# Moving the waits for a q tile's six loads from the first max matmuls to the o products ahead of them

## The chip, the cores and the metric

The kernel runs on one core of one Trainium2 chip. The metric is the device time of one execution in microseconds (us); lower is better. The time before is a median over three runs. One further execution was taken with the hardware profiler, and all durations below are read from its trace.

Five engines work in parallel, each with its own in-order stream of instructions: PE (matmuls, with its weight loads shown as a row of their own, PEld), DVE (vector), ACT (activations), POOL and SP, which here only issues DMAs. They are held together by semaphores. An instruction of PE can carry one semaphore to wait for. Where it depends on more, the build puts one or two instructions ahead of it in PE's stream that do nothing but wait; the trace shows them as EVENT_SEMAPHORE in the row PEldq.

## The reference, cut to what matters

The output mixes two branches of the same input x (1 x 2048 x 640) by a gate g = sigmoid(x . gate_w):

```
def _A_ref(x, wq, wk, wv, wo):            # 32 heads of 20, one k and one v for all heads
    ...
    scores = jnp.einsum("bhqd,bkd->bhqk", q, k) * (Dh ** -0.5)
    p = _softmax(scores, axis=-1)
    o = jnp.einsum("bhqk,bkd->bhqd", p, v)
    return (...o...) @ wo
def _B_ref(x, w1, b1, w2, b2):            # an MLP across the tokens
    h = _layernorm(x, axis=-1)
    u = _gelu(jnp.einsum("bsd,sf->bdf", h, w1) + b1)
    y = jnp.einsum("bdf,fs->bds", u, w2) + b2
    ...
return g * a + (1 - g) * b
```

Branch A is the larger part of the work: for every query and head a row of 2048 scores, its maximum, its exponentials and the product of these with v.

## The kernel before, in words

**Tiles.** A q tile holds 512 queries of four heads; there are NU = 32 of them. It is a pair of rows of blocks in SBUF: partitions 0 to 59 for two of the heads and 64 to 123 for the other two (three copies of 20 rows each, high, low and high part of q). `load_q(n)` fills it by six DMAs, which `part` issues on SP's queue (line 148), three for each half of the partitions. Each tile is used twice. First come its *max tiles* (`ms_next`, line 506): 64 matmuls of 128 queries by 512 keys, 32 with each half of the partitions, whose row maxima DVE takes (line 514). Later come its *score tiles* (`qk`, line 688), 128 keys by 512 queries, whose exponentials ACT writes to SBUF (line 700). Between the two the maxima go through DRAM and into two spare rows of the tile. So a tile's loads and the first max matmul of each half are tied by three DMA semaphores.

**Stretches and bursts.** The program is built in `n_st` stretches. A stretch j takes 8 score tiles, some 8 or 9 max tiles and a share of other work (the MLP's matmuls, lines 1008 and 836, later the product with wo, line 961), and places these on two lanes, the upper and the lower 64 rows of the array, whose matmuls run side by side. The order comes from `arrange`, `layout` and the cost model in `issue`; it is fixed when the program is built. After each stretch but the first, `burst` multiplies the exponentials of the two units of the previous stretch with v: eight matmuls at line 721 (`pv_mm`), which use all 128 rows and four column tiles of 32. They accumulate in one bank that ACT then copies out. PE alternates stretch, burst, stretch, burst.

**Waits.** `touch` (line 464) records by hand which instruction wrote or read a PSUM bank or a region of exponentials, and adds only the waits that follow from that. The waits for q tiles aren't in it; the framework adds them to the first instruction that reads the loaded rows.

**How many max tiles a stretch gets.** `wants[j]` plus what the last stretch left over; the two halves share them so that they keep in step (lines 1228 to 1235). `given[b]` counts the max tiles handed out for each half, so `given[b] // 32` is the q tile that half b is at.

In this text, the k-th burst is counted from 0, and the stretch after it has the same number.

Of the kernel before, what the change touches and what calls it, by code (L numbers as in the profile page):

```python
# [19 lines left out]
S, D, H, DH, F = 2048, 640, 32, 20, 1728  # L20
# [19 lines left out]
def mix_kernel(ctx: ExitStack, tc: tile.TileContext, A_x, A_wq, A_wk, A_wv, A_wo,  # L40
               B_x, B_w1, B_b1, B_w2, B_b2, gate_w, out):
    nc = tc.nc
    x = A_x[0]
    y_out = out[0]

    def f32(ap):
        return ap.bitcast(F32)
# [84 lines left out]
    def load_q(n):  # L132
        if n in FIFTH[:2]:
            t = w1b[3].rearrange("p r c f -> p r (c f)")
        elif n == 29:
            t = pools["q5"] = pools["last"].tile([P, 2, NB], F32R, name="q5")
        elif n in FIFTH or n in (6, 11, 16, 21, 26, 31):
            t, at = (slot[1], 2 * DC * D + 2 * D) if n in FIFTH else (slot[0], 2 * FC * HD2)
            t = t[:, at:at + 2 * NB].rearrange("p (r q) -> p r q", r=2)
        else:  # L140
            t = qp.tile([P, 2, NB], F32R, name="q")
        qb, g = divmod(n, NQ)
        cols = slice(qb * NB, (qb + 1) * NB)

        def part(b, j, src):
            o = 64 * b + DH * j
            rows = q_scr[src, g * 4 * DH:(g + 1) * 4 * DH, cols]
            nc.sync.dma_start(out=f32(t[o:o + DH]), in_=rows.rearrange("(a b d) q -> b d a q", a=2, b=2)[b])

        parts = [lambda b=b, j=j, src=src: part(b, j, src) for b in range(2) for j, src in enumerate((0, 1, 0))]  # L150
        if one_by_one[0]:
            q_parts_due.extend(parts)
        else:
            for f in parts:
                f()
        return t

    qtiles = {}
    one_by_one, q_parts_due = [False], []

    def new_q(n):
# [11 lines left out]
    with tc.tile_pool(name="pa", bufs=1) as pa, \  # L173
# [22 lines left out]
        for c in range(DC):  # L196
            nc.sync.dma_start(out=xin[0][:, :, c * P:(c + 1) * P],
                              in_=x[:NB, c * P:(c + 1) * P].rearrange("(t p) d -> p t d", p=P))
# [6 lines left out]
        for c in range(DC):  # L205
# [5 lines left out]
                          in_=B_b1[:(FC - 1) * P].rearrange("(c p) -> c p", p=P))  # L211
# [93 lines left out]
        def q_parts(m, ts):  # L305
            cols = slice(m * P, (m + 1) * P)
            return [[(wq_hi[:, c, cols], ts[c][0]) for c in range(DC)],
                    [(wq_hi[:, c, cols], ts[c][1]) for c in range(DC)],
                    [(wq_lo[:, c, cols], ts[c][0]) for c in (0, 3, 1, 4, 2)]]
# [88 lines left out]
        for sb in range(NQB):  # L398
# [11 lines left out]
            for m in range(DC):  # L410
# [3 lines left out]
                p = q_parts(m, ts)  # L414
# [46 lines left out]
    turns, xs, pre = [0], [], []  # L461
    writer, readers, engines = {}, {}, set()

    def touch(ins, reads=(), writes=()):
        need = []
        for r in reads:
            need.append(writer[r])
            readers.setdefault(r, []).append(ins)
        for w in writes:
            need += readers.pop(w, [])  # L470
            writer[w] = ins
        for n in {n.ins.name: n for n in need}.values():
            tc.add_manual_dep(ins.ins, n.ins.name, SYNC, reason="a bank or a p region used again")
        me = str(ins.ins.engine)
        engines.add(me)
        for e in engines - {me}:
            tc.declare_no_dep(ins.ins, group=e, keep=[n.ins for n in need], reason="other banks and p regions")
        tc.add_to_no_dep_group(me, ins.ins)

    def bank(i):  # L480
        return span(i, 1) if i < 7 else xs[2]
# [7 lines left out]
    given = [0, 0]  # L489
    issued = [0, 0]  # L490

    def ms_next(b):
        k = given[b]
        if k >= 32 * NU or k // 32 not in qtiles:
            return None
        given[b] += 1
        n, r = divmod(k, 32)
        (kq, pr), qt = divmod(r // 4, 2), r % 4

        def step(i=None):  # L500
            if n not in mtiles:
                mtiles[n] = mpool.tile([P, 16, 4], F32, name="mp")
            if i is None:
                turns[0] += 1
            ms = pre[turns[0] % 4].tile([P, NB], F32, name="x" if turns[0] % 4 else "g") if i is None else bank(i)
            mm = nc.tensor.matmul(ms, qtiles[n][64 * b:64 * b + 60, pr, qt * P:(qt + 1) * P],  # L506
                                  kst[64 * b:64 * b + 60, kq * NB:(kq + 1) * NB], start=True, stop=True)
            region = [("x", i)] if i is not None else []
            if region:
                touch(mm, writes=region)  # L510
            out = mtiles[n][:, (2 * b + pr) * 4 + qt, kq:kq + 1]

            def reduce():
                red = nc.vector.tensor_reduce(out, ms, axis=AX.X, op=ALU.max)  # L514
                if region:
                    touch(red, reads=region)
                issued[b] += 1

            return reduce

        return step
# [85 lines left out]
    with tc.tile_pool(name="psb", bufs=2, space=PSUM, side="right") as psb, \  # L607
# [13 lines left out]
        for fc in range(PRO):  # L621
            pu = [psb.tile([P, NB], F32, name=f"pu{r}") for r in range(2)]
            for hf in range(4):
# [4 lines left out]
                for c in range(HS):  # L628
                    st = hf * HS + c
                    for k, (w, h) in enumerate(((wh, h_hi[0]), (wh, h_lo[0]), (wl, h_hi[0]))):  # L630
                        for r in range(2):
                            rows = slice(64 * r, 64 * r + 64)
# [82 lines left out]
    osum = {}  # L715
    later = []

    def pv_mm(u, o, first, last, i):
        for hh in range(4):
            j = ptiles.pop((u, hh))  # L720
            mm = nc.tensor.matmul(o[32 * hh:32 * hh + 32, :], v_sb[:, units[u][1], :], p_all[:, j * NB:(j + 1) * NB],  # L721
                                  start=first, stop=last, skip_group_check=True)
            touch(mm, [("p", j)], [("x", i)])
            p_left[j // 4] -= 1
            if not p_left[j // 4]:
                p_free.append(j // 4)
# [316 lines left out]
    ph = [(rows[1 - b], rest if b else [], done if b else []) for rows, rest, done in seq for b in range(2)]  # L1043
    assert len(ph) == n_st
    first_use, last_use = {}, {}
    for i, (fs, _, _) in enumerate(ph):
        for f in fs:
            c = getattr(f, "chunk", None)
# [6 lines left out]
    for c in range(4 * PRO + 4, len(chunks)):  # L1055
        b = min((b for b in range(4) if b < 3 or last_use[c] < begin or over[3] >= ending - 1), key=lambda b: over[b])
# [10 lines left out]
    X_US, F_US, O_US = 0.2345, 0.1468, 0.869  # L1067
# [12 lines left out]
    def next_free():  # L1080
        return min(range(len(free)), key=lambda i: free[i])
# [102 lines left out]
    def burst(us):  # L1184
        i = next_free()
        t = max(max(lane) + FIRST_US, state["last"] + LAST_US, free[i]) + len(us) * O_US
        o = bank(i)
        for u in us:
            pv_mm(u, o, u == us[0], u == us[-1], i)
            fetch_at(u)  # L1190
        collect(us[-1], o, i)
        each, hold = EACH["act"]
        free[i] = spend("act", each, t + 0.25) - each + hold
        lane[:] = [t + NEXT_US] * 2
        fresh[:] = [True, True]
# [15 lines left out]
    wants = [8 + (len(fs) > 22) for fs, _, _ in ph]  # L1211
# [5 lines left out]
    left, n = 64 * NU - 16 - sum(given) - sum(wants[:at]), n_st - at  # L1217
    wants[at:] = sorted(left * (i + 1) // n - left * i // n for i in range(n))
    assert sum(given) + sum(wants[:n_st - 8]) >= 64 * (NU - 1)
    owed = 0  # L1220
    for j in range(n_st):
        h, i = j % 2, j // 2
        due, stores[:] = stores[:], []
        blocks = [], []
        ss = [lambda at, u=u, pr=pr: qk(u, pr, h, at, blocks[u % 4 // 2], pairs.get(2 * (u % 4) + pr, 1))
              for u in range(4 * i, 4 * i + 4) for pr in range(2)]
        fs, rest, done = ph[j]
        to = owed + wants[j]
        own = round((min(to, 9) + F_US / X_US * len(fs) - len(ss)) / 2)
        if h:  # L1230
            own = (given[0] - given[1] + to + 1) // 2
        own = min(to, max(0, own))
        before = sum(given)
        ms = [[f for f in (ms_next(x) for _ in range(c)) if f] for x, c in ((h, own), (1 - h, to - own))]
        owed = to - (sum(given) - before)
        pop_chain()
        arrange(h, ss, *ms, fs, done)
        if j % 8 == 7:
            u = j // 8
            for n in (u + 3, u + 4) if u == 0 else (u + 4, u + 5) if u == 1 else (u + 5,):  # L1240
                if n != 29:
                    new_q(n)
        for f in due:
            f()
        if follow:
            follow.pop(0)()
        if not follow and not (j + 1 < n_st and len(ph[j + 1][0]) == 20):
            n = len(row_max)
            follow += ms_done()
            if follow:  # L1250
                follow.pop(0)()
                follow.append(lambda n=n: store_max(n))
        settle()
        pop_chain()
        w1_load(fetched[0] + 3)
        for f in rest:
            f()
        spend("dve", 0.03)
        spend("act", 0.1)
        if j == 8 * 25 - 1:  # L1260
            new_q(29)
        if j == n_st - 3:
            raw = last_wo()
        if j == n_st - 1:
            w_last = split_last(raw)
        if j:
            burst((2 * j - 2, 2 * j - 1))
# [150 lines left out]
    for st, d in held:  # L1418
        oT, _ = room(jobs.index((st, CUT, HEAD)))
        for c in range(DC - 1, CUT // P - 1, -1):  # L1420
            r = min(P, HEAD - c * P)
            for j, w in ((0, wo_hi), (1, wo_hi), (0, wo_lo)):
                a, new = acc_at(st, d)
# [35 lines left out]
```

## Time and profile before

| what | value |
|---|---|
| runs | 1618.53 us median (1618.27 to 1618.7) |
| profiled execution | 1618.5 us, of which the span from first to last instruction 1616.5 us |
| granted TensorE clock | 0.999 |
| PE busy | 1608.8 us of the span |
| DVE busy | 1383.9 us |
| ACT busy | 1261.1 us |
| bursts | 255, the first at 189.0 us |

A row of the windows view gives, for one stretch of time, the busy time of each engine with the number of its instructions, then the granted clock, the mean busy share of the DMA engines and what they moved in GB/s. Windows here run from the start of one burst to the start of the next, so their length is the period of a burst and its stretch. In the timeline a row gives start, duration, engine, line, operation and count; rows of the same kind that follow each other are merged. The instructions that only wait don't count as busy; the view of one line lists them.

### The profile page before, as it was taken

The page shows a single profiled execution, that of the slowest core. Times are in us where ns is not written, and L with a number is a line of the kernel's source. Part 1 is how long each engine was busy: PE and PEld are TensorE (multiplying, and loading weights), DVE is VectorE, ACT ScalarE, POOL GpSimd, SP SyncE. Part 2 cuts the span into 40 slices and gives each one's busy share as a digit, 9 for nine tenths or more (in the row PEclk, how much of TensorE's full clock was granted, in tenths as well). Part 3 has the DMA queues.
Part 4 walks back from the last instruction along what each step waited for, and adds up shares of the span by engine and source line. Part 5 has one row for each costly group of instructions (what it writes and reads, how often), then busy time and mean ns, then how long its engine had stood idle before and what let it go on. Part 6 is the DMA issues. An engine that isn't in the chain of part 4 may idle for free.

```text
span 1616.5 us, 39520 instructions
## 1 busy us (share of the span) xinstructions
PE 1608.8 (100%) x14868; PEld 1123.3 (69%) x14868; DVE 1383.9 (86%) x2629; ACT 1261.1 (78%) x2350; POOL 841.1 (52%) x927
## 2 busy tenths in 40 slices
PE   9999999999999999999999999999999999999998
PEld 7899876776776776666666666666666666666665
DVE  6689899999999999888888888888888886567754
ACT  4545677777777778878888788887888879999976
POOL 6567766777787776554554334444444433333321
PEclk9999999999999999999999999999999999999999
DMA  7665322232222232222212121112221113333221
GB/s 215 206 168 144 87 66 73 61 77 69 69 70 74 53 76 63 74 68 69 69 47 64 35 61 54 58 54 60 61 60 47 54 37 112 103 115 98 85 83 59
DMA packets 180308, 129.27 MB, mean 80 GB/s; under 512 B 41585, under 2 KB 150030, under 8 KB 180118
## 3 DMA queue, kind: packets, MB, share of 16 engines
q1 hardware_dynamic: 179830, 126.43, 27.7%
q8 instruction: 117, 1.92, 0.5%
q14 instruction: 73, 0.60, 0.1%
q10 hardware_dynamic: 288, 0.33, 0.1%
HBM read 93.57 MB, written 32.15 MB: 78 GB/s over the span
## 4 chain that ended last, share of the span: by engine, by line
PE 98%; POOL 0%; DVE 0%; DMA 0%; issue 0%; ACT 0%; POOLq 0%; SPq 0%; DVEq 0%
PE xs L721 29%; PE xs L688 18%; PE xs L506 18%; PE g L836 11%; PE g L1008 7%; PE pp L302 4%; PE pu L633 4%; PE g L961 3%; PE xs L910 1%; PE x L506 1%; PE pt L294 0%; PE pp L366 0%; PE xs L1424 0%; PE pp L191 0%; PE g L688 0%
## 5 line engine op out<-in xcount | busy, mean ns | idle before, releaser
L514 DVE TENSOR_REDUCE mp<-xs 128x1 f32<-128x512 f32 x1943 | 1196.9, 684 | 154.7 <-PE xs L688 78.4
L700 ACT ACTIVATE p<-xs 128x512 f32<-128x512 f32 (+1 forms) x1834 | 1011.7, 680 | 10.9 <-PE xs L688 6.4
L743 POOL TENSOR_TENSOR osum<-osum,part 128x512 f32<-128x512 f32 x212 | 274.2, 1294 | 604.8 <-ACT part L742 597.9
L721 PE MATMUL xs<-p,v_sb 128*32 128x512 f32 x4096 | 492.3, 598 | 0.0
L688 PE MATMUL xs<-q,kst 62*128 62x512 f32 x1339 | 476.2, 417 | 1.3 <-ACT p L700 1.3
L506 PE MATMUL xs<-kst,q 60*128 60x512 f32 x1242 | 437.4, 416 | 0.0
L688 PEld LDWEIGHTS xs<-q,kst 62*128 62x128 f32 x1339 | 235.9, 185 | 74.6 <-DVE mp L514 52.3
L742 ACT ACTIVATE part<-xs 128x512 f32<-128x512 f32 x212 | 126.8, 598 | 199.6 <-PE xs L721 197.3
L1008 PE MATMUL g<-slot,w 64*128 64x320 f32 x1728 | 266.8, 306 | 0.0
L721 PEld LDWEIGHTS xs<-p,v_sb 128*32 128x32 f32 x4096 | 106.9, 109 | 225.5 <-issue 161.0
L506 PEld LDWEIGHTS xs<-kst,q 60*128 60x128 f32 x1242 | 209.6, 184 | 73.4 <-DVE mp L514 44.4
L1008 PEld LDWEIGHTS g<-slot,w 64*128 64x128 f32 x1728 | 259.1, 184 | 1.9
L127 POOL TENSOR_TENSOR w<-wr,w 128x512 fp32r<-128x512 f32 (+1 forms) x180 | 225.5, 1255 | 34.5 <-ACT w L124 22.1
L688 PE MATMUL xs<-slot,kst 62*128 62x512 f32 x567 | 206.9, 418 | 0.4 <-DVE row L922 0.2
L506 PE MATMUL xs<-kst,slot 60*128 60x512 f32 x573 | 205.3, 418 | 0.0
L836 PE MATMUL g<-u,w 64*128 64x320 f32 x1296 | 201.7, 306 | 0.0
L836 PE MATMUL g<-slot,w 64*128 64x320 f32 x1296 | 201.5, 306 | 0.0
L836 PEld LDWEIGHTS g<-u,w 64*128 64x128 f32 x1296 | 195.6, 184 | 1.7
L836 PEld LDWEIGHTS g<-slot,w 64*128 64x128 f32 x1296 | 195.6, 184 | 1.5
L688 PEld LDWEIGHTS xs<-slot,kst 62*128 62x128 f32 x567 | 99.7, 185 | 31.7 <-DVE mp L514 22.6
L506 PEld LDWEIGHTS xs<-kst,slot 60*128 60x128 f32 x573 | 96.2, 184 | 33.1 <-DVE mp L514 20.4
L961 PE MATMUL g<-slot 64*128 64x320 f32 x660 | 106.7, 306 | 0.0
(197 smaller groups left out, 1483.7 us busy)
## 6 DMA issues: line engine op xcount, KB each, us to landing
wr<-in_B_w_dram SPq DMA_DIRECT2D x155, 256.0 KB
q<-q_scr SPq DMA_DIRECT2D x126, 80.0 KB
rb<-r_scr SPq DMA_DIRECT2D x120, 64.0 KB
slot<-o_scr SPq DMA_DIRECT2D x22, 320.0 KB
y_scr<-yo SPq DMA_DIRECT2D x16, 320.0 KB
q_scr<-qh SPq DMA_DIRECT2D x19, 256.0 KB
q_scr<-ql SPq DMA_DIRECT2D x19, 256.0 KB
o_scr<-rb SPq DMA_DIRECT2D x120, 40.0 KB
```

The source lines that it names most:

```text
L127: nc.gpsimd.tensor_sub(wl, wr, f32(wh))
L302: nc.tensor.matmul(pp, w, t, start=first and n == 0, stop=not more and n == len(steps) - 1)
L506: mm = nc.tensor.matmul(ms, qtiles[n][64 * b:64 * b + 60, pr, qt * P:(qt + 1) * P], kst[64 * b:64 * b + 60, kq * NB:(kq + 1) * NB], start= ...
L514: red = nc.vector.tensor_reduce(out, ms, axis=AX.X, op=ALU.max)
L688: mm = nc.tensor.matmul(s, kst[64 * b:64 * b + 62, kb * P:(kb + 1) * P], q[64 * b:64 * b + 62, pr, :], start=True, stop=True)
L700: act = nc.scalar.activation(p_all[:, a * NB:(j + 1) * NB], s, AF.Exp, scale=SCALE)
L721: mm = nc.tensor.matmul(o[32 * hh:32 * hh + 32, :], v_sb[:, units[u][1], :], p_all[:, j * NB:(j + 1) * NB], start=first, stop=last, skip_g ...
L742: touch(nc.scalar.activation(part, o, AF.Copy), [("x", i)])
L743: nc.gpsimd.tensor_add(osum[n], osum[n], part)
L836: other_tile(half, nc.tensor.matmul(hold["p"][:, :HD2], w[r, fc % HS, :], u[d][r, fc, :], start=(hold["n"] == 1), stop=(hold["n"] == 6 * F ...
L961: other_tile(half, nc.tensor.matmul(hold["p"][:, :HD2], o[r, c, :], w[r, c, d * HD2:(d + 1) * HD2], start=(hold["n"] == 1), stop=(hold["n" ...
L1008: other_tile(half, nc.tensor.matmul(hold["p"][:, :HD2], w[r, st % HS, :], h[d][r, st, :], start=(hold["n"] == 1), stop=(hold["n"] == 6 * NS)))
```

## The change

A burst asks which q tile the max tiles of the next stretch reach. If that tile's loads were not waited for by an earlier burst, the six DMAs of `load_q` are handed to the burst's first six matmuls, one each. Nothing is added to the work, and the order of all matmuls, of all other engines' instructions and of all DMAs stays as it was: only waits move. To know the next stretch's max tiles ahead, the rule that splits them between the halves is put into a function, `share`, with the same result.

```
-            nc.sync.dma_start(out=f32(t[o:o + DH]), in_=rows.rearrange("(a b d) q -> b d a q", a=2, b=2)[b])
+            ins = nc.sync.dma_start(out=f32(t[o:o + DH]), in_=rows.rearrange("(a b d) q -> b d a q", a=2, b=2)[b])
+            q_loads.setdefault(n, []).append(ins)
...
-    def touch(ins, reads=(), writes=()):
-        need = []
+    def touch(ins, reads=(), writes=(), also=()):
+        need = list(also)
...
+    arrived = []
+
     def pv_mm(u, o, first, last, i):
...
-            touch(mm, [("p", j)], [("x", i)])
+            touch(mm, [("p", j)], [("x", i)], [arrived.pop(0)] if arrived else [])
...
         o = bank(i)
+        if len(wants) > us[1] // 2 + 2:
+            counts = share(us[1] // 2 + 2)
+            n = max((given[b] + counts[b] - 1) // 32 for b in range(2))
+            if n in qtiles:
+                arrived.extend(q_loads.pop(n, ()))
         for u in us:
             pv_mm(u, o, u == us[0], u == us[-1], i)
```

PE's stream at one of the places, burst 120 and the stretch after it, shows it. `xs` are banks, `kst` holds the keys, `slot_80` is here the memory of q tile 19, `p` the exponentials; names such as DMAHW3_49 are semaphores, and several in one row mean that EVENT_SEMAPHORE instructions stand ahead. First the burst and the places of the tile's first use, before; a row marked "..." leaves rows out:

```order
L721 MATMUL xs_2757<-p,v_sb 32x512 [waits Activation_49]
L721 MATMUL xs_2757<-p,v_sb 32x512 x7
L688 MATMUL xs_2761<-q,kst 128x512 [waits DVE_49]
...
L506 MATMUL xs_2757<-kst,slot_80 128x512 [waits DMAHW3_49,DMAHW4_49,DMAHW2_49,Activation_49]
...
L506 MATMUL xs_2761<-kst,slot_80 128x512 [waits Activation_49]
L506 MATMUL xs_2761<-kst,slot_80 128x512 [waits DMAHW6_49,DMAHW7_49,DMAHW5_49,DVE_49]
L721 MATMUL xs_2761<-p,v_sb 32x512 [waits Activation_49]
```

The first half of the tile is first read in the middle of the stretch, the second half by the very last matmul of the stretch. The same places now:

```order
L724 MATMUL xs_2757<-p,v_sb 32x512 [waits DMAHW2_49,Activation_49]
L724 MATMUL xs_2757<-p,v_sb 32x512 [waits DMAHW3_49]
L724 MATMUL xs_2757<-p,v_sb 32x512 [waits DMAHW4_49]
L724 MATMUL xs_2757<-p,v_sb 32x512 [waits DMAHW5_49]
L724 MATMUL xs_2757<-p,v_sb 32x512 [waits DMAHW6_49]
L724 MATMUL xs_2757<-p,v_sb 32x512 [waits DMAHW7_49]
L724 MATMUL xs_2757<-p,v_sb 32x512 x2
...
L507 MATMUL xs_2757<-kst,slot_80 128x512 [waits Activation_49]
...
L507 MATMUL xs_2761<-kst,slot_80 128x512 [waits DVE_49]
L724 MATMUL xs_2761<-p,v_sb 32x512 [waits Activation_49]
```

The six DMA waits stand on the burst's matmuls, with one EVENT_SEMAPHORE ahead of the first, and the four ahead of the max matmuls are gone. In the whole program PE's stream has 278 instructions that only wait before and 198 now: 104 are gone and 24 are new. 29 of the 255 bursts carry such waits: bursts 0, 7, 14, 20, 26, 32, 39, 46, 52, 58, 64, then every eighth from 72 to 192, and 202 and 218.

More of the change, by code (lines that the diff above doesn't have):

```diff
@@ L156, in load_q @@
         return t
-    qtiles = {}
+    qtiles, q_loads = {}, {}
     one_by_one, q_parts_due = [False], []
@@ L1220, in mix_kernel, with share @@
     owed = 0
+    def share(j):
+        h, to = j % 2, owed + wants[j]
+        own = round((min(to, 9) + F_US / X_US * len(ph[j][0]) - 8) / 2)
+        if h:
+            own = (given[0] - given[1] + to + 1) // 2
+        own = min(to, max(0, own))
+        return (to - own, own) if h else (own, to - own)
     for j in range(n_st):
@@ L1227, in mix_kernel @@
         fs, rest, done = ph[j]
[L1228 to L1235, printed above, removed]
+        counts, before = share(j), sum(given)
+        ms = [[f for f in (ms_next(x) for _ in range(counts[x])) if f] for x in (h, 1 - h)]
+        owed = sum(counts) - (sum(given) - before)
         pop_chain()
```

## The prediction

> **What bounds the kernel now.** I read the page first, for the engine that sets the span.
>
> ```profile
> span 1616.5 us, 39520 instructions
> ...
> PE 1608.8 (100%) x14868; PEld 1123.3 (69%) x14868; DVE 1383.9 (86%) x2629; ACT 1261.1 (78%) x2350; POOL 841.1 (52%) x927
> ...
> PE 98%; POOL 0%; DVE 0%; DMA 0%; issue 0%; ACT 0%; POOLq 0%; SPq 0%; DVEq 0%
> ```
>
> The chain that ended last is PE almost throughout, but a busy PE says little here: two lanes run side by side, and a matmul that is held on one lane hides behind the other. The period from burst to burst tells more. So next I took the windows view over one cycle of stretches in the middle of the kernel, from burst 120 to burst 128 and one more, and over two stretches of the first part and two of the part around 1350 us.
>
> ```profile
> core 0: us, PE busy (x) PEld busy (x) DVE busy (x) ACT busy (x) POOL busy (x), PEclk, DMA share, GB/s
> 893.75:899.43 5.68, 5.68 (x53) 3.90 (x53) 5.07 (x12) 4.57 (x9) 0.00 (x0) 1.00 0.33 94
> 899.43:905.10 5.67, 5.67 (x54) 3.85 (x54) 5.10 (x10) 4.43 (x9) 1.94 (x4) 1.00 0.01 3
> 905.10:910.68 5.58, 5.58 (x54) 3.72 (x53) 5.03 (x12) 4.85 (x10) 1.30 (x1) 1.00 0.02 1
> 910.68:916.25 5.57, 5.57 (x54) 3.73 (x52) 5.09 (x11) 4.45 (x9) 2.70 (x3) 1.00 0.22 50
> ...
> 921.83:927.50 5.67, 5.67 (x55) 3.83 (x53) 5.08 (x9) 4.55 (x9) 2.80 (x3) 1.00 0.01 2
> 927.50:933.08 5.58, 5.58 (x53) 3.72 (x53) 4.86 (x11) 4.85 (x10) 4.93 (x6) 1.00 0.57 191
> ...
> 938.65:944.34 5.69, 5.69 (x54) 3.91 (x52) 5.07 (x12) 4.58 (x9) 0.00 (x0) 1.00 0.34 96
> ```
> ```profile
> 364.69:370.75 6.06, 6.06 (x59) 4.28 (x58) 6.06 (x13) 4.45 (x9) 5.06 (x6) 1.00 0.00 1
> ...
> 467.71:473.90 6.19, 6.19 (x61) 4.45 (x59) 6.18 (x13) 5.46 (x11) 4.96 (x7) 1.00 0.63 171
> ...
> 1350.40:1355.02 4.62, 4.62 (x45) 2.90 (x44) 3.15 (x8) 4.48 (x10) 1.29 (x1) 1.00 0.22 76
> ...
> 1359.62:1364.24 4.62, 4.62 (x44) 2.90 (x43) 3.01 (x7) 4.50 (x11) 2.09 (x3) 1.00 0.58 177
> ```
>
> Three parts have three limits. In the first, DVE is busy for the whole period (6.06 of 6.06). In the last, ACT is busy 4.48 to 4.50 of 4.62. In between neither DVE (5.03 of 5.58) nor ACT (4.85) is full, and the period is 5.57 or 5.58 us except in three stretches of each eight. The first of the three, after bursts 120 and 128, is where a q tile is first used: 5.68 and 5.69 us.
>
> **What the first use costs now.** The view of line 506 lists the instructions that only wait; the first two rows are for the stretch after burst 120, the third for the whole trace, the fourth is line 688's, over the whole trace too.
>
> ```profile
> L506 PEld LDWEIGHTS xs<-kst,slot x6: 183/184/187, 896.6 to 899.0; 60*128 60x128 f32 x6
> ...
> L506 PEldq EVENT_SEMAPHORE  x4: 51/51/51, 895.6 to 898.9; - x4
> ...
> L506 PEldq EVENT_SEMAPHORE  x115: 51/51/51, 97.3 to 1429.4; - x115
> ...
> L688 PEldq EVENT_SEMAPHORE  x64: 51/51/51, 177.1 to 1565.0; - x64
> ```
>
> Each takes 51 ns, all its DMAs having landed long before. The four stand in two pairs. The weight loads in the timeline tell which pair costs something; the first five rows are the start and end of the stretch after burst 120, the last two the end of the one after burst 122, which has none.
>
> ```profile
> 895.60 0.18 PEld L688 LDWEIGHTS xs<-q,kst 62*128 62x128 f32 x1 [0.84 <-DVE mp L514]
> ...
> 898.42 0.19 PEld L688 LDWEIGHTS xs<-q,kst 62*128 62x128 f32 x1
> 898.44 0.33 PEld L836 LDWEIGHTS g<-u,w 64*128 64x128 f32 x2
> 898.82 0.37 PEld L506 LDWEIGHTS xs<-kst,slot 60*128 60x128 f32 x2
> 899.43 0.16 PEld L721 LDWEIGHTS xs<-p,v_sb 128*32 128x32 f32 x8 [0.24 <-ACT p L700]
> ```
> ```profile
> 910.18 0.19 PEld L506 LDWEIGHTS xs<-kst,slot 60*128 60x128 f32 x2
> 910.67 0.16 PEld L721 LDWEIGHTS xs<-p,v_sb 128*32 128x32 f32 x8 [0.30 <-ACT p L700]
> ```
>
> The first pair runs at 895.6, when the stretch's first load starts; the load that it guards, the first of the new tile in `slot`, comes at 896.6. PE's stream is ahead of the array there, and the pair is hidden. The second pair stands right ahead of the stretch's last matmul, which reads the second half of the tile. There the two loads of line 506 cover 0.37 us, in the other stretch 0.19: the last load comes 0.18 us later. From the first of the two to the burst are 0.61 us against 0.49: 0.12 of it reaches the burst.
>
> **The change, part by part.**
>
> *Removed: the second pairs of the middle part.* One window for each of its 16 first uses (bursts 72, 80, ... 192), the first, the last and the sum:
>
> ```profile
> 624.21:629.85 5.64, 5.64 (x54) 3.91 (x53) 5.08 (x12) 4.57 (x9) 2.28 (x4) 1.00 0.34 97
> ...
> 1297.90:1303.59 5.69, 5.69 (x55) 3.91 (x53) 5.08 (x12) 4.58 (x9) 0.00 (x0) 1.00 0.59 174
> sum 91.15, PE 91.15 PEld 62.55 DVE 81.38 ACT 73.39 POOL 2.28; mean PE 5.70 PEld 3.91 DVE 5.09 ACT 4.59 POOL 0.14
> ```
>
> 91.15 - 16 x 5.58 = 1.87 us. Once the pair is gone, ACT's last exponential is late next: in the stretch after burst 122 the burst waits for it already (0.30 us "ACT p L700"), which is what makes 5.58. So 5.58 is as far as these stretches come.
>
> *Removed: the first pairs,* hidden as shown: 0. If their cover were gone they would cost what the second pairs do, 0.12 each, but nothing moves there.
>
> *Removed elsewhere.* In the first part, the stretch of the trace with the four waits (after burst 46) is long, 6.19 us, but DVE is busy 6.18 of it, so it is DVE's own work that fills it: I take 0. If its excess over 6.06 went, that would be 0.13; a gain of 0.2 is the upper end for this part. In the last part the stretch with the first use has 4.62 us like that without: 0.
>
> *The excess of the second stretch of each eight.* 5.67 after burst 121. The same 5.67 stands after burst 125, where no q tile is near, so I take it for the work that ends there, and 0. Were it left over from the delay before it, 16 x 0.09 = 1.4 us more would go; that is the far end of the gain.
>
> *Added: an EVENT_SEMAPHORE ahead of 24 bursts.* It stands ahead of the burst's first matmul, which waits for ACT anyway: PEld sits idle 0.24 to 0.30 us before the burst until ACT's exponential ends. 51 ns fit in that: 0. Without that cover, 24 x 0.05 = 1.2 us.
>
> *Added: the waits on the second to sixth matmul.* Behind each stand, in PE's order, the rest of the burst and the next stretch, and ACT, which copies the burst's bank out. What do they cost when the semaphore has long been reached? The trace has no burst with DMA waits inside. The nearest rows are those of the last burst of all, which takes four units and whose tenth, twelfth, fourteenth and sixteenth matmul carry a wait for ACT (the four loads each at 1602.46 and 1603.32 begin with matmuls nine to twelve and thirteen to sixteen).
>
> ```profile
> 1601.60 0.13 PEld L721 LDWEIGHTS xs<-p,v_sb 128*32 128x32 f32 x4 [0.30 <-issue]
> ...
> 1602.46 0.13 PEld L721 LDWEIGHTS xs<-p,v_sb 128*32 128x32 f32 x4 [0.30 <-issue]
> ...
> 1603.32 0.13 PEld L721 LDWEIGHTS xs<-p,v_sb 128*32 128x32 f32 x4 [0.30 <-issue]
> ```
>
> Four loads take 0.13 us with two waits among them and without. I take 0. The upper end is the 51 ns that a wait costs as an instruction of its own. Only the waits up to the fourth matmul count, since the four column tiles run side by side and the fifth follows the first on its tile 0.43 us later (two groups from 1601.60 to 1602.46, 0.86 us). These are 75 in 25 bursts, 4 in bursts 26 and 32 and 1 in burst 0: 80 x 0.051 = 4.1 us.
>
> *Will the DMAs have landed a burst earlier?* The burst now waits where the max matmuls waited, up to a period sooner.
>
> ```profile
> L148 SPq DMA_DIRECT2D slot<-q_scr x6: 273/336/419, 877.0 to 883.0; - x6
> ...
> L148 SPq DMA_DIRECT2D q<-q_scr x6: 318/334/336, 224.4 to 226.3; - x6
> ...
> 231.45:237.58 6.13, 6.13 (x61) 4.40 (x59) 6.13 (x13) 4.92 (x10) 4.52 (x6) 1.00 0.47 77
> ...
> 891.00:893.70 2.70, 2.70 (x29) 2.38 (x26) 2.68 (x6) 2.70 (x6) 1.19 (x1) 1.00 0.01 3
> ```
>
> The tile of burst 120 is issued by 883.0, and the DMA engines are idle from 891.0 (share 0.01) to the burst at 893.75. The closest case is burst 7, at 231.45, the last of whose loads is issued at 226.3, 5.1 us ahead. I take 0; a landing later than the burst would cost that one burst the difference.
>
> *Sum:* -1.87 us and nothing against it. The profiled execution took 1618.5 us (span 1616.5 and 2.0 around it), the median of the runs is 1618.53, so both give 1616.6 us, 0.12% less. A difference under 0.2% (3.2 us) counts here as none, about what a measurement of this kernel can tell.
>
> **The rivals.**
>
> 1. *The waits in the burst cost as much as waits of their own: slower.* At the second pairs two semaphores delay a load by 0.18 us, 0.09 each. 80 waits at that price are 7.2 us; less 1.87 that is 5.3 more: 1623.8. At 51 ns each the loss is 4.1 - 1.87 = 2.2: 1620.7, still within 0.2%. From (3.24 + 1.87) / 80 = 0.064 us a wait it is slower by over 0.2%. Against it speak the rows of the last burst; for it, that those waits came late in a burst, when PE's stream was ahead, while here the first matmul is held by ACT until the moment that it starts. [...]
> 2. *No gain.* The last matmul of the stretch comes sooner, but the burst then meets something else: 1618.5. For it: DMA traffic is high in these stretches (share 0.33 to 0.59). Against it: the stretch from 927.50 has a share of 0.57 and yet 5.58.
> 3. *More gain.* If also hidden pairs cost half the price, 0.05 an instruction, the net 80 fewer make 4.0 us: 1614.5. For it: the second stretch's 5.67. Against it: the stretch with 4.62 us.
>
> **How the numbers follow.** The forecast has 0.68. Rival 2 has 0.12, rival 1 has 0.06 at the small price and 0.09 at the large one, rival 3 has 0.05. Faster by over 0.2% is rival 3, slower is rival 1 at the large price, the rest, 0.86, is within 0.2%. The range goes from 1615.0, the forecast with the far ends of its gains (1.87 + 0.2 + 1.4 = 3.5), to 1618.7, rival 2 with the slowest run before. It leaves out rival 3 (0.05) and both prices of rival 1 (0.15).
>
> **What the changed profile would show.** Windows of 5.58 us after bursts 72, 80, ... 192, with a sum near 89.3 instead of 91.15. Bursts whose first row is still eight loads in 0.16 us; 0.3 or more there, or a period in which the stretch is short and the burst long, is rival 1. A burst that begins later than ACT's exponential, because of the EVENT_SEMAPHORE ahead, would show as idle time put down to DMA. If the loads at the stretch's end move up by 0.18 us and the period stays at 5.68, it is rival 2, and the releaser of the burst tells what came next. The prediction is wrong if a wait that is fulfilled holds a matmul in a column tile, which no row of this trace excludes.

## The result, and the profile after

| | before | changed |
|---|---|---|
| median of 20 runs | 1618.54 us (1617.93 to 1618.94) | 1615.95 us (1615.51 to 1616.44) |
| span of the profiled execution | 1616.5 us | 1614.6 us |

The ratio of the changed kernel's time to that before is 0.9984, with a 95% interval of 0.9978 to 0.999: 2.6 us, or 0.16%, are gone. The forecast was 1616.6 us, 1.9 us less. The measured gain is clear of noise and larger than the forecast by 0.7 us.

The page of the changed kernel shows the same work: PE's matmuls, DVE's and ACT's instructions in the same number, and 80 instructions fewer in all (39520 before).

```profile
span 1614.6 us, 39440 instructions
...
PE 1606.7 (100%) x14868; PEld 1119.8 (69%) x14868; DVE 1383.9 (86%) x2629; ACT 1261.2 (78%) x2350; POOL 841.2 (52%) x927
```

The windows view over the 16 first uses of a q tile in the middle part (bursts 72, 80, ... 192) shows where the time went; the rows are those of bursts 72 and 120 and the sum.

```profile
624.73:630.25 5.52, 5.52 (x55) 3.74 (x53) 4.96 (x11) 4.46 (x9) 2.29 (x4) 1.00 0.34 96
...
893.45:899.02 5.57, 5.57 (x55) 3.74 (x53) 4.96 (x12) 4.46 (x9) 0.00 (x0) 1.00 0.33 96
...
sum 89.01, PE 89.01 PEld 59.71 DVE 79.17 ACT 71.26 POOL 2.29; mean PE 5.56 PEld 3.73 DVE 4.95 ACT 4.45 POOL 0.14
```

The sum was 91.15 us, so 2.14 us come from these stretches. The next two windows, after bursts 121 and 122, and those after bursts 7 and 46 in the first part, answer the other terms:

```profile
232.06:238.09 6.03, 6.03 (x59) 4.27 (x58) 6.03 (x13) 4.82 (x10) 4.41 (x6) 1.00 0.59 89
468.30:474.37 6.07, 6.07 (x60) 4.29 (x59) 6.06 (x13) 5.34 (x11) 4.90 (x6) 1.00 0.67 169
899.02:904.68 5.66, 5.66 (x55) 3.84 (x54) 5.20 (x12) 4.54 (x9) 1.94 (x4) 1.00 0.01 3
904.68:910.26 5.58, 5.58 (x54) 3.74 (x53) 5.04 (x12) 4.86 (x10) 1.30 (x1) 1.00 0.02 1
```

The stretches without a first use are as they were (5.66 against 5.67, 5.58 both times). After bursts 7 and 46 there are 6.03 and 6.07 us where 6.13 and 6.19 stood: 0.10 and 0.12 less. Together that is 2.14 + 0.22 = 2.4 us. No other stretch that the change touches differs by more than 0.03 us between the two traces.

The weight loads at the end of the stretch after burst 120 and at the start of the burst itself, in the timeline:

```profile
893.45 0.16 PEld L724 LDWEIGHTS xs<-p,v_sb 128*32 128x32 f32 x8 [0.30 <-ACT p L701]
...
898.53 0.19 PEld L507 LDWEIGHTS xs<-kst,slot 60*128 60x128 f32 x2
899.02 0.16 PEld L724 LDWEIGHTS xs<-p,v_sb 128*32 128x32 f32 x8 [0.30 <-ACT p L701]
```

The last two max loads of the stretch cover 0.19 us, as in a stretch without a first use, where they covered 0.37; the next burst starts 0.49 us after the first of them, as there. The burst that carries six DMA waits starts with eight loads in 0.16 us like any other, after the same 0.30 us of waiting for ACT. In the trace, the bursts last 1.92 us in both kernels.

### The profile page after: what moved, and what is told of

Its sections match the earlier page's. It is cut to its first block, busy times and chain, and to the rows that moved or that the text cites. A ratio compares the mean times of both kernels' runs of the same rounds, so it can differ in the third digit from the quotient of the medians.

```text
span 1614.6 us, 39440 instructions
## 1 busy us (share of the span) xinstructions
PE 1606.7 (100%) x14868; PEld 1119.8 (69%) x14868; DVE 1383.9 (86%) x2629; ACT 1261.2 (78%) x2350; POOL 841.2 (52%) x927
## 3 DMA queue, kind: packets, MB, share of 16 engines
q8 instruction: 117, 1.92, 0.5%
## 4 chain that ended last, share of the span: by engine, by line
PE 97%; SPq 1%; DMA 1%; DVE 0%; POOL 0%; issue 0%; ACT 0%; POOLq 0%; DVEq 0%
PE xs L724 30%; PE xs L689 18%; PE xs L507 17%; PE g L839 11%; PE g L1011 7%; PE pu L634 4%; PE pp L303 3%; PE g L964 3%; PE xs L913 1%; PE x L507 1%; DMA xa<-in_A_x_dram 0%; PE pt L295 0%; PE xs L1436 0%; SPq L200 0%; DVE st L236 0%
```

## The experiments

Theory A: an instruction that only waits costs time where PE's stream doesn't stand ahead of the array, and the only such place is right ahead of a stretch's last matmul. Theory B: each such instruction costs its share wherever it stands, 2.6 us for 80. In most of the runs the two theories lie about 0.1% of the time apart or less, which the medians can hardly part; so for every run the sum of the 16 windows is given too, 91.15 us before and 89.01 us in the changed kernel. A comparison of medians is with the kernel before, run beside it.

**Half of the waits each.** Only the loads of the second half of the tile are handed to the burst (the first run), or only those of the first half (the second run, with `b == 0`).

```
-            q_loads.setdefault(n, []).append(ins)
+            if b == 1:
+                q_loads.setdefault(n, []).append(ins)
```

> The burst waits only for the three loads of the tile's second half; the waits for the first half stay in the middle of the stretch. Theory A (only the two instructions right ahead of the stretch's last matmul cost anything): the whole gain is here, 16 stretches go from 5.70 to 5.57 on average, and the kernel takes 2.1 to 2.6 us less than before, near 1616.1. Theory B (each instruction that only waits costs its share wherever it stands, 2.6 us for 80, 0.03 us each): PE's stream has 29 fewer than before, so 0.9 us less, near 1617.6.

> The burst waits only for the three loads of the tile's first half; the two instructions ahead of the stretch's last matmul stay. Theory A: no gain, 1618.5 within 0.3, and the 16 windows still sum to about 91.1 us. Theory B: 25 fewer instructions, 0.8 us less, near 1617.7.

The first run took 1616.37 us, ratio 0.9985 (0.9976 to 0.9993), the second 1618.01 us, ratio 0.9997 (0.9989 to 1.0006). The sums of their windows, the first run's above:

```profile
sum 89.02, PE 89.02 PEld 59.70 DVE 79.17 ACT 71.27 POOL 2.31; mean PE 5.56 PEld 3.73 DVE 4.95 ACT 4.45 POOL 0.14
```
```profile
sum 90.88, PE 90.88 PEld 62.55 DVE 81.06 ACT 73.13 POOL 2.30; mean PE 5.68 PEld 3.91 DVE 5.07 ACT 4.57 POOL 0.14
```

The second half alone gives the whole gain of the 16 stretches, the first half 0.27 us of it. Theory A holds and theory B falls: of two kernels with 29 and 25 instructions fewer, one gains eight times what the other does in these stretches. The second run's median alone would not say so: it is 0.8 us below that of the kernel beside it, what theory B gave and more than theory A's 0.3, though its interval includes no difference. In its trace the stretches from which waits went are only some 0.4 us shorter. Of the 0.27 us, 0.09 each are those of two stretches, after bursts 104 and 160; these come back at the end of the text, where a run shows that they are no price of the first half's waits as such.

In the first part, two instructions stand right ahead of the last max matmul in the stretches after bursts 7 and 46 only. After burst 7 the halves come in the other order, so that the first half is the one that the last matmul reads. The windows after these two bursts, the first run's above:

```profile
231.18:237.30 6.12, 6.12 (x61) 4.40 (x59) 6.12 (x13) 4.91 (x10) 4.51 (x7) 1.00 0.57 87
467.48:473.55 6.07, 6.07 (x61) 4.28 (x59) 6.05 (x13) 5.33 (x11) 4.92 (x6) 1.00 0.65 174
```
```profile
231.12:237.16 6.04, 6.04 (x61) 4.27 (x59) 6.04 (x13) 4.83 (x10) 4.43 (x6) 1.00 0.48 78
467.34:473.53 6.19, 6.19 (x60) 4.46 (x59) 6.17 (x13) 5.46 (x11) 4.95 (x7) 1.00 0.59 174
```

After burst 46 the gain is the second half's, after burst 7 the first half's. So it is the place in the stretch that costs, and not which half of the tile is waited for.

**The middle of the stretch instead of the burst.** All six waits on the tile's first max matmul; the burst carries none.

```
-                arrived.extend(q_loads.pop(n, ()))
+                pass
...
-                touch(mm, writes=region)
+                touch(mm, writes=region, also=q_loads.pop(n, ()))
```

> The burst carries no DMA wait; all six stand on the tile's first max matmul, in the middle of the stretch (three instructions ahead of it). Theory A: the middle is as good a place as the burst, since PE's stream is about 1 us ahead there; the kernel takes 1616.0 and the 16 windows sum to 89.0 us. A rival on the burst (the gain needs the burst's free slots): the third instruction delays the middle of the stretch, and part of the 2.1 us comes back. Theory B: 26 fewer instructions, 0.8 us less, near 1617.7.

It took 1615.9 us, ratio 0.9982 (0.9973 to 0.9991), and its windows sum to the same as the changed kernel's:

```profile
sum 89.00, PE 89.00 PEld 59.71 DVE 79.17 ACT 71.25 POOL 2.29; mean PE 5.56 PEld 3.73 DVE 4.95 ACT 4.45 POOL 0.14
```

So the burst isn't needed for the gain. What counts is that the waits are no longer at the end of the stretch.

**All six on the burst's first matmul,** with three instructions ahead of it, and **on its second**, with the same three between the first matmul and the second. The first of the two edits, and the second:

```
-            touch(mm, [("p", j)], [("x", i)], [arrived.pop(0)] if arrived else [])
+            touch(mm, [("p", j)], [("x", i)], arrived)
+            arrived.clear()
```
```
-            touch(mm, [("p", j)], [("x", i)], [arrived.pop(0)] if arrived else [])
+            also = arrived if hh == 1 else []
+            touch(mm, [("p", j)], [("x", i)], also)
+            del also[:]
```

> All six waits on the burst's first matmul: three instructions that only wait ahead of it, and none on matmuls two to six. Theory A, with the cover of the burst's wait for ACT (0.24 to 0.30 us of idle time, and the load before it some 0.4 us earlier): the three are hidden, the kernel takes as much as the changed one, 1616.0. If the cover is too short, each of 24 bursts begins up to 0.1 us later and 2.4 us are lost again: 1618.4. Theory B: 24 fewer than before, 0.8 us less, near 1617.7.

> As the changed kernel, but all six waits on the burst's second matmul: three instructions that only wait between the first matmul, which ACT holds until it starts, and the second. Theory A (what counts is whether the stream stands ahead of the array at that place): here it doesn't, the other three column tiles start about 0.3 us later, the bursts with such waits grow from 1.92 to 2.2 us, and some 25 of them cost 7 us: near 1623. Rival C (a fulfilled wait is free anywhere in a burst): 1616.0, bursts of 1.92 us.

On the first matmul: 1615.73 us, ratio 0.9982 (0.9973 to 0.9991), and a sum of 88.98 us. On the second: 1623.68 us, ratio 1.0031 (1.002 to 1.0043), and a sum of 93.77 us. The timeline of burst 120 in the latter, and the instructions that only wait in it:

```profile
897.61 0.14 PEld L724 LDWEIGHTS xs<-p,v_sb 128*32 128x32 f32 x2 [0.30 <-ACT p L701]
897.94 0.23 PEld L724 LDWEIGHTS xs<-p,v_sb 128*32 128x32 f32 x7 [0.20 <-DMA l_scr<-osum]
```
```profile
L724 PEldq EVENT_SEMAPHORE  x3: 51/51/51, 897.6 to 897.9; - x3
```

The first matmul's loads come at 897.61, and the next only at 897.94, 0.33 us later: three times 0.11. (The releaser in the second row is only the DMA whose semaphore moved last.) In the trace most such bursts of the middle part last 2.24 us instead of 1.92 (this one 2.28), and the 16 periods are 0.30 us longer each than in the changed kernel: (93.77 - 89.01) / 16. So the same three instructions cost nothing one place further ahead (88.98 us against 89.01), where PE waits for ACT in any case (0.30 us in the changed kernel), and 0.3 us behind it. A wait that is fulfilled and that a matmul itself carries is free here, as the changed kernel shows (bursts of 1.92 us with five such matmuls and without); rival 1's mechanism appears as soon as the waits become instructions of their own between the burst's matmuls.

**More and fewer at the end of the stretch.** In the kernel before, the loads of one half are cut into two of 10 partitions each, so that its first max matmul waits for six DMAs and three instructions stand ahead where two did: for the second half in the first run, for the first half in the second (`b == 0`).

```
-            nc.sync.dma_start(out=f32(t[o:o + DH]), in_=rows.rearrange(...)[b])
+            w = DH // 2 if b == 1 else DH
+            for r in range(0, DH, w):
+                nc.sync.dma_start(out=f32(t[o + r:o + r + w]),
+                                  in_=rows.rearrange(...)[b][r:r + w])
```

> The kernel before, but each of the three loads of a tile's second half is cut into two of 10 partitions: six semaphores for that half, so three instructions that only wait ahead of the stretch's last matmul where two were (22 more in all). Theory A: one more at that place costs half of what two did, 0.06 us in each of 16 stretches: 1.0 us slower, near 1619.5; the 16 windows sum to about 92.1 us instead of 91.15. Theory B (0.03 us for each instruction anywhere): 0.7 us slower, near 1619.2, spread over all first uses.

> The same, but the loads of the first half are cut: three instructions instead of two ahead of the first max matmul, in the middle of the stretch, and as many more DMAs as in the run beside it. Theory A: hidden, no change, 1618.5 within 0.3, the 16 windows still sum to 91.1 us. Theory B: 0.7 us slower, near 1619.2. If the extra DMAs cost something by themselves, both runs show it.

The first took 1620.89 us, ratio 1.0014 (1.0005 to 1.0023), the second 1618.79 us, ratio 1.0002 (0.9993 to 1.0011). Their sums:

```profile
sum 92.59, PE 92.59 PEld 62.58 DVE 82.66 ACT 74.83 POOL 2.29; mean PE 5.79 PEld 3.91 DVE 5.17 ACT 4.68 POOL 0.14
```
```profile
sum 90.98, PE 90.98 PEld 62.58 DVE 81.06 ACT 73.22 POOL 2.28; mean PE 5.69 PEld 3.91 DVE 5.07 ACT 4.58 POOL 0.14
```

The place decides again: a third instruction costs something at the end of the stretch only. But its price is (92.59 - 91.15) / 16 = 0.09 us, or 0.10 beside the second run's 90.98, which has as many DMAs, and not the 0.06 that I expected from half of two. So the first run came out 1.4 us above theory A's 1619.5. The rest of that is in other stretches: both traces have some 0.6 us more in five of the middle part (four are longer, one is shorter), alike in the two. The added DMAs are what the two runs share and the place of the waits is not, so I put it down to the DMAs, which no run tried alone.

Two cost 0.12 us beside none, by the run that moved only the first half's waits, (90.88 - 89.01) / 16, and a third 0.10. So I tried one: the burst takes five loads, and the sixth, of the second half, stays where it was.

```
-            q_loads.setdefault(n, []).append(ins)
+            if (b, j) != (1, 2):
+                q_loads.setdefault(n, []).append(ins)
```

> As the changed kernel, but the burst takes only five of the six loads; the sixth stays with the second half's first max matmul, so that one instruction that only waits stands ahead of the stretch's last matmul, where the kernel before has two and the run with six loads of that half has three. Those two cost 0.12 and 0.22 us a stretch beside none. Theory A1 (0.11 us each, of which the first 0.1 us is covered, since the matmul's lane isn't free sooner): one costs nearly nothing, the 16 windows sum to 89.0 to 89.3 us, the kernel takes 1616.0. Rival A2 (in proportion, 0.06 each): the windows sum to 90.0 us, the kernel takes 1617.0.

It took 1616.22 us, ratio 0.9985 (0.9976 to 0.9994), with a sum of 89.16 us: (89.16 - 89.01) / 16 = 0.01 us for one. A1 holds. The last two max loads of the stretch after burst 120, with three, two and one instruction ahead of the second (two: the kernel before):

```profile
899.35 0.50 PEld L509 LDWEIGHTS xs<-kst,slot 60*128 60x128 f32 x2
```
```profile
897.90 0.25 PEld L508 LDWEIGHTS xs<-kst,slot 60*128 60x128 f32 x2
898.40 0.16 PEld L725 LDWEIGHTS xs<-p,v_sb 128*32 128x32 f32 x8 [0.25 <-ACT p L702]
```

The pair covers 0.50, 0.37 (in the prediction) and 0.25 us, and 0.19 with none: each further instruction moves the load by 0.12 to 0.13 us, the first by 0.06. And with one, the burst still starts 0.50 us after the first load, as with none (0.49). What it waits for shows in the exponential that the profile names as its releaser, here with none (the changed kernel, burst at 899.02) and with two (the kernel before, burst at 899.43):

```profile
898.33 0.64 ACT L701 ACTIVATE p<-xs 128x512 f32<-128x512 f32 x1
```
```profile
898.62 0.65 ACT L700 ACTIVATE p<-xs 128x512 f32<-128x512 f32 x1
```

With none it ends 0.05 us before the burst, with one 0.06, but with two 0.17 and with three 0.3 us, although the profile puts the idle time down to ACT in each case. With one, two and three the burst starts 0.42 to 0.43 us after the last max load. So with none ACT sets the start, with two and three the last max matmul does, and with one both come to nearly the same moment: the cover at this place is about as long as one instruction. The stretch after burst 46, in the first part, says the same: it takes 6.07, 6.08, 6.19 and 6.30 us with none, one, two and three instructions ahead of its last max matmul.

## Why the prediction was right

**The place of the cost.** The step that told the first pairs from the second by the weight loads, and gave the whole gain to the second, was right: handing over the second half alone gives all of the 2.14 us of the 16 stretches, and the first half alone almost none.

**The 16 stretches, -1.87 us.** Measured -2.14. The floor was mis-sized: I took 5.58 us from stretches without a first use and said that these stretches come no further, but they come to 5.56 on average, and to 5.52 after burst 72. That the burst then waits for ACT was right: the exponential ends 0.05 us before it. Before the change the same entry (0.24 us "ACT p L700") did not mean that, since ACT had ended 0.17 us before. A floor from another kind of stretch was good to 0.02 us only, 0.3 us in all. What makes the 0.02 us isn't shown; it isn't ACT's amount of work alone, since the stretch after burst 123 has 4.45 us of it, as these have, and takes 5.57.

**"Removed elsewhere", 0.** This step failed. After bursts 7 and 46, 0.10 and 0.12 us went, together just above the upper end of 0.2 that I had given for this part. I had looked at burst 46 alone, and burst 7's stretch has the four waits too. And I had argued that DVE is busy for the whole period, so that its own work fills it. Its rows for the stretch after burst 46, before, in the view of line 514 and in the timeline:

```profile
L514 DVE TENSOR_REDUCE mp<-xs x12: 679/681/691, 467.0 to 473.7; 128x1 f32<-128x512 f32 x12
```
```profile
467.04 1.89 DVE L514 TENSOR_REDUCE mp<-xs 128x1 f32<-128x512 f32 x3
...
468.85 5.56 DVE L514 TENSOR_REDUCE mp<-xs 128x1 f32<-128x512 f32 x9
```

Each lasts 0.68 us, but three take 1.89 us and not 2.04, and nine 5.56 and not 6.1: the records overlap, and one starts about every 0.60 us. Of the twelve, ten start inside the period of 6.19 us, so DVE needs about 6.0 us of it (ten times 0.60, my estimate) although it reads as busy for 6.18. There was room for the 0.12 us that went; after the change the same ten start in 6.07 us.

**The second stretch of each eight, 0.** Right: it has 5.66 us still.

**The waits in the burst and the instruction ahead of it, 0.** Right: the bursts last as long as before, 1.92 us, to within 0.01 us; the run with all six on the first matmul (88.98 us against 89.01) shows that even three instructions fit under the wait for ACT (0.30 us in the changed kernel). Rival 1 named the doubt well (the first matmul is held until the moment that it starts), but what it feared needs waits that stand as instructions of their own behind that matmul. Its price of 0.09 us took the second pair for two semaphores; these are two instructions, and with the one that the matmul carries they wait for four (four semaphores stand on it in the order, and the view of line 506 has four instructions for the two such matmuls of the stretch). The instructions' own records show 51 ns, and where nothing covers them, behind the burst's first matmul, they cost 0.11 us each (three: 0.33), about twice that.

**Rivals 2 and 3.** Nothing else was met at the stretch's end. Taking away hidden pairs gave nothing: the stretches after bursts 20, 39, 52, 58 and 64, whose waits stand further ahead in the stretch, are as long as before to 0.02 us.

**The sum.** 2.14 + 0.22 makes 2.4 us of the 2.6 in the medians; the difference of 0.2 us is inside the interval (0.1% to 0.22% of 1618.5 us, 1.6 to 3.6 us). Two other differences between the two traces lie where the change moves no wait: the first burst comes 0.6 us later in the profiled execution after, and the stretch after burst 246 is 5.26 us long in that of before and 5.02 after. That stretch begins with a load that waits for a DMA (`slot<-m_scr`, for which PE sat idle 0.2 us in the trace of before and not in that of after), and in the traces of all the experiments it is as short as after, also in the two that keep all the old waits. So I take the 5.26 us for this one execution's; no second trace of the kernel before shows it.

## What to carry to other kernels

An instruction that only waits cost nothing here while its engine's stream stood ahead of the engine (the 16 windows sum to 88.98 to 89.02 us in the four kernels whose waits for a tile all stand there), and 0.11 us where it did not, less what other waits covered there (0.01 us was left for a single one at the stretch's end): look where the next weight load comes, not at how many there are. When a matmul depends on several DMAs that landed long ago, let an earlier matmul pick the waits up one by one, in the middle of dense work or ahead of a wait that stands there anyway, but never as instructions behind a matmul that is held, where three cost 0.30 us in each of the 16 periods. And a period in which another engine reads as busy throughout (DVE here, 6.18 of 6.19 us) doesn't say that this engine sets it; look first at how far apart its records start (0.60 us, where each lasts 0.68).

## What the runs showed of the hardware that I had not expected

The cost of several instructions in a row isn't in proportion: 0.01 us for one, 0.12 for two and 0.22 for three at the end of these stretches. A cover comes off once: one instruction moves the last max load by 0.06 us, to about the moment at which ACT lets the burst start in any case, and each further one moves the burst, by 0.10 to 0.11 us.

In the kernel before, the stretch after burst 104 was 5.77 us long and not 5.68, and its last two max loads were further apart than elsewhere with the same two instructions between them; in the run that moved only the first half's waits they are not (before, then that run):

```profile
808.77 0.46 PEld L506 LDWEIGHTS xs<-kst,q 60*128 60x128 f32 x2
```
```profile
808.41 0.36 PEld L508 LDWEIGHTS xs<-kst,q 60*128 60x128 f32 x2
```

So the same two instructions cost 0.09 us more at this place. The stretch after burst 160 did the same. It isn't simply the two instructions some twenty matmuls ahead of them that make it: these are gone in the run above, but in the run that has three in their place the loads are as close, and the two stretches take 5.68 and 5.69 us:

```profile
808.78 0.37 PEld L509 LDWEIGHTS xs<-kst,q 60*128 60x128 f32 x2
```

What makes the 0.09 us, and whether it lies in where the instructions come in the stream, no run here tells.
